# An attention and squared-ReLU kernel: seven products in place of eight for the second half batch and for the last two token tiles, and turned distance blocks as weights

## The chip, the cores and the metric

The kernel runs on one core of one Trainium2 chip. A core has five engines with a queue each: PE (TensorE, matrix products into PSUM; its weight loads are shown apart as PEld), DVE (VectorE), ACT (ScalarE), POOL (GpSimd, which here only issues transfers) and SP (SyncE, which issues transfers too). The metric is the device time of one launch in microseconds. A measurement is the median of several executions; one more execution is profiled, and its trace is what the views below are read from.

## What is computed

Attention with a linear distance penalty, a local window of 96 positions and 8 global keys, and behind it a feed-forward layer with a squared ReLU. 4 batches, 8 heads of 64, 768 positions, 2048 hidden columns:

```python
scores = q @ k.T / 8 - slopes[h] * dist          # dist: |i - j|, 96 for a global key outside the window
scores = where(is_global | is_local, scores, -1e9)
a = softmax(scores)
x = (a @ v) with the heads side by side          # 3072 x 512
h = maximum(x @ w_in, 0)                         # 3072 x 2048
out = (h * h) @ w_out                            # 3072 x 512
```

## The kernel before

**Halves.** The work is cut into eight half batches of 384 tokens (`halves[0]` to `halves[7]`, three token tiles of 128 each). Each goes through attention, which leaves the turned tokens `x.xt` (512 x 384), then the first layer, which leaves the squared hidden values `x.h2` (16 hidden tiles of 128 x 384), then the second layer. Halves 0 and 1, the first batch, are worked through tile by tile in an opening of their own (`OPENING`, a list of short names: `P` distances, `S` scores, `A` attend, `X` turn into `x.xt`, `F`/`G` first layer of half 0, `E`/`D` of half 1). All later halves run their attention beside the two layers of the half before.

**Scores of the first batch.** For the first three tiles `distances` (line 1391) lays the penalty into PSUM ahead of the scores: for each of 8 heads a matmul with a scaled identity `slope_id` as weights and a 128-column block of `dmask16` as the moving side. `score_tile` adds the scores on top, and one exponential follows. For the other tiles the exponential is multiplied with a ready `mask` on DVE.

**Seven products in place of eight.** From half 2 on the first layer is computed in groups (`layer1_group`, line 913): two input blocks of 256 rows, two halves of 192 tokens, and two sets of two hidden tiles (m and m+8) make a 2 x 2 by 2 x 2 block product, done with seven products of four 192-column matmuls instead of eight. Four groups cover the 16 hidden tiles; `LETTERS` and `LAYER1` say in which order their products stand. For this, sums of w_in blocks are made once (`list_in_mix`, line 876, which needs all four chunks of w_in), sums of token blocks for each half (`list_x_mix`, line 898), and in between PSUM banks are copied out or handed from one product to the next: three copies (the one into a second bank, `seed`, and two `hold`), two relus and two `add_relu` for each group. The second layer does the same with two token tiles together (`layer2_pair`, line 1117): seven products of eight 256-column matmuls, with sums of hidden tiles (`mix_tokens`, line 1074, whole or in two parts by `WIDE`) and of w_out blocks (`list_mix`, line 561).

In the kernel before, half 0 and half 1 do the first layer plainly (`layer1`), half 1's second eight hidden tiles at 384 columns each. Of the 24 token tiles, 22 go in 11 pairs; the first tile of half 0 and the last of half 1 go plainly (`layer2`, line 1049: 16 matmuls of 512 columns each).

**What sets the order.** Every operation is put on record in a `Plan` with the operations that it needs, and `ORDER`, a table written out, says on which engine and at which place each one is issued: `p12` is the PE job with index 12, `l` a load on POOL, `a`, `d`, `g`, `s` any other operation on ACT, DVE, POOL or SP. Engines work through their own queues in that order, and waits between engines are put in by the framework from the data. `LOADING` says in which order the loads of the first batch and of w_in (`c0` to `c3`, 512 hidden columns each) are put on record; `ORDER` has the last word. Each of the eight PSUM banks is given out by the plan.

The pairs and the second layer of half 0 and half 1 are listed in the loop at line 1594:

```python
if hb == 1:
    main = l1(x1, range(8, NFT)) + l2(w, 0)
    pairs = [((w, 1), (w, 2)), ((x, 0), (x, 1))]
...
if hb == 1 and GROUPS:
    side.append((8 * 0.65, list_in_mix))
if hb == 1:
    for i, job in enumerate(l2(x, 2)):
        main.insert(len(main) - 3 + i, job)
```

Of the kernel before, what the change touches and what calls it, by code (L numbers as in the profile page):

```python
# [14 lines left out]
P = 128  # L15
# [3 lines left out]
K4 X11 A20 X00 K5 X10 A21 S4o S4b S3b X21 X20 F1 G11 V2 S5o V3 S5b G10 F0 A40 V4 A30 G01 A41  # L19
A31 G00 G30 X41 F3 X30 X31 A50 X40 F2 A51 E11 G31 G20 X50 G21 X51 E01 E10 D0 E00 D1"""  # L20
# [3 lines left out]
LOADING = """v1 k3 k2 q2 v0 q3 q4 q5 k5 v2 k4 c1 v3 c0 v4 v5 c3 c2"""  # L24
# [12 lines left out]
WIDE = [0, 1, 1, 1, 0, 1, 1, 1, 0, 0, 0]  # L37
# [3 lines left out]
LAYER1 = {2: "abcdAeBfCgD1E2F3G4h5i6j7klmn", 3: "abcdAeBfCgD1E2F3G4h5i6j7klmn",  # L41
# [7 lines left out]
ORDER = """d1 g2 a4 s8 p0 s10 a6 d12 a0 d13 l2 l1 a18 l3 d3 a30 d17 d15 d20 l4 a25 d14 a29 d9 a16 l0 d19 a26  # L49
d22 d21 d5 a23 p2 a28 l10 d11 p1 a24 p5 d7 l5 p3 l6 p10 d31 a32 a33 d34 l9 p6 a27 d35 p9 a39 p8 l8  # L50
d44 p11 d36 a40 p7 d43 l7 p4 a46 p13 d37 a41 p14 d45 l11 p12 d48 a42 p16 p17 d59 a47 l12 p15 a52 p25
d51 p19 l13 a49 d38 p28 p24 d55 a53 p20 l14 d69 p23 d64 a50 p34 d65 a60 l16 p31 d56 p21 a81 p22 d72
p27 l15 a61 p29 d58 p30 a57 p26 d70 a82 p33 l17 d68 p18 a71 a77 p35 d66 l23 p36 p32 d54 a86 d67 a85
p40 d62 p39 l18 d63 a97 d91 a73 p41 l19 d84 a78 d83 a74 p37 d79 l20 a98 d75 p44 l22 p38 d107 l21 d80
p47 d76 a89 p52 p48 d96 l27 a92 d111 p42 a93 l28 d106 a112 p43 l29 a119 p46 a113 d105 p45 a101 l30
d110 p53 d103 p55 p50 a120 p59 a90 d95 d116 a87 d100 p51 d99 d94 p57 d122 p54 d125 p65 p63 p49 d135
d121 p67 d146 a114 d128 a102 p61 p62 a104 d132 d117 a88 p75 d108 a129 p83 d115 a142 d109 p60 d209
a143 d118 d189 p64 a130 d273 d193 a138 p70 a136 p72 d159 p82 a133 d194 p71 d187 a134 p56 d160 a131
d190 a162 p69 d137 a186 p81 d161 l33 a123 d212 p74 d139 a165 d163 l25 a188 d156 p84 d205 a166 l31
d151 p73 a169 a184 d157 p85 l35 d206 a164 d167 a171 d147 p58 a168 l36 d196 p80 d124 l34 a126 p89  # L60
d148 p88 a181 p86 l32 d210 a202 d150 a182 p76 l24 d158 a170 d183 p77 a172 l26 d152 p87 a203 d174
a199 l37 p78 d154 a197 p79 p66 d204 a200 l38 a127 d207 p68 d185 a178 d149 a179 p90 a140 d180 p91
a213 d208 a175 d144 p94 a173 d201 a176 p92 d153 s220 d237 p100 a215 d195 a155 p102 s221 d211 d238
a214 p96 a224 d177 p95 a241 a141 p98 d225 p104 a216 s198 d226 p93 p97 a246 d223 a217 s227 a218 p103
d230 d222 p99 s231 a245 d240 p110 d239 p108 s219 l43 p111 a256 d244 a249 l44 p106 a257 d259 a250
d236 l40^227 p109 d247 p116 d228 p101 a252 l45 d251 a269 d258 p115 l41 a270 p114 d242 p113 a253 d192
l42 a262 d255 p117 a265 d232 p105 l46 d191 a272 a260 d233 p123 a266 l48^220 p118 a263 d280 p121 p122
d235 a274 l39 d234 p132 a278 d268 p128 a145 d279 p130 a287 d264 p126 a292 p127 d271 p125 a290 s327
p134 a285 d267 p139 d286 p135 d283 p133 a302 p136 s248 l47 d254 a295 p129 d296 s328 p143 a288 d293
p141 a284 p138 d297 p142 d304 p140 a289 p124 d300 s229 p137 a303 d294 p120 a306 d281 p146 a305 p144  # L70
d277 p147 a311 p131 a301 d307 p107 s282 d298 a329 p145 d291 p148 a309 p112 a308 d312 a399 d314 p151
p152 d313 p156 l51^282 s299 a330 p149 d310 p119 d315 a331 d322 a341 p150 s243 d316 a333 s261 l49^231
d275 a342 p168 d317 p165 a321 l52 a334 p153 d318 p155 a355 l53 a336 d332 p154 a337 d323 l50 d319
a359 p170 d324 l54 p160 d320 a361 p172 a350 p174 d338 a364 p161 p163 d366 a351 p164 a326 p176 d325
d340 p166 d436 p158 d369 a354 d335 a339 p169 a347 d356 p178 a367 p157 d360 p159 a371 d343 a344 p171
d348 a345 p181 d353 p180 s402 l56^327 a362 p182 a375 d374 p173 a372 p184 d346 p186 s403 a365 p162
d376 a357 p188 a382 d352 p192 d363 a380 p167 p179 a385 d391 s276 p175 s377 a373 p189 d358 a368 p190
a404 p185 d386 p193 s392 d388 d381 p183 p191 d393 a387 p187 l63 d389 p196 a383 p177 d390 a413 l59
p194 d378 a370 d384 a414 l74 p201 d379 a409 p202 p195 a423 l58 p199 d405 a426 d415 l62 p198 a427
d406 a424 d395 l55^377 p206 a410 d407 p200 a437 d416 l61^403 a421 d396 p211 a411 d408 p197 a420 l60  # L80
d397 p203 d481 p212 a417 d429 p204 a422 l75 d425 a445 a418 d484 p207 l66 d412 p205 a444 a438 d433
l57 a430 p213 d428 p216 d435 a446 d400 p220 l65 s434 a431 p214 p219 a455 d447 p215 a454 p227 d450
a448 s496 p222 d398 p225 d485 p218 a449 d486 p217 a461 d432 p210 a464 s497 a452 d419 a458 p224 d482
p231 a401 d460 p228 p229 d465 s349 l64 p221 a442 a453 p226 d466 p235 d456 p232 a462 p223 d469 a475
p239 d483 a451 d467 a571 p234 d459 a457 p208 p233 d473 a489 p237 a494 p209 d470 s474 a471 p230 d439
p241 a468 d440 a498 p242 s394 d478 s443 a500 s441 d463 p236 p238 d476 p249 a479 d472 p245 p244 a517
p240 d488 a501 d487 a505 p247 d499 a506 d477 l73^441 s495 a508 p246 d513 a518 d492 l71 d480 a509
p258 p248 d490 a533 l70 d511 p243 d519 p251 a514 l69 d491 a515 d520 p252 a502 p265 l72 p262 d542
a503 p260 p253 a538 l67 d536 p270 a525 p266 d507 a527 p267 l68 a543 d510 p257 a528 p268 d548 a532
p255 p271 d544 a530 p261 d493 a549 p273 d545 a546 p259 d537 p269 a552 p274 d534 p275 d516 p264 p276  # L90
a540 d547 p278 a556 p272 d554 a553 p254 a550 d535 s575 p250 a551 d559 d504 p282 s576 d521 p283 a565
p279 d523 a529 p281 a524 p277 d522 a563 p284 p286 d566 d560 p287 d568 a578 a567 d557 p280 p291 a564
d541 s558 d555 p263 d577 p285 p256 s526 d561 s512 p293 d583 a531 d569 p295 d595 a602 d539 p296 p292
a604 d570 a605 p298 d598 a596 a607 s597 p288 d599 s562 a608 p290 d606 p294 a585 d601 a586 p301 s574
d579 a592 d600 s573 a603 p297 a617 d609 p289 d614 p303 a588 d610 s584 d587 a593 s572 p306 a611 d580
d619 p307 a612 d623 p299 a589 d663 p310 p308 a615 d582 a624 d613 p300 d664 a625 p304 a629 p315 d590
a616 p312 d591 a621 p323 d581 d631 a635 p309 p302 a645 d627 p311 a618 p329 d630 p316 a628 p319 d594
p317 a636 p313 d640 p327 d637 a632 p305 a653 p321 d638 a650 p333 d622 a642 p322 p330 a644 d659 p320
p318 d654 p314 s660 a639 p325 d633 p326 a648 p332 d634 p335 s626 d658 s655 p324 d649 p331 d646 p334
p336 d656 a661 d641 a643 p328 p346 a667 d668 p351 a651 d682 p338 d657 a698 a692 d670 p353 d669 p355  # L100
d671 p357 d703 p337 a706 d665 a652 p361 d701 p350 a674 d711 p347 a672 p359 a673 d666 p363 p339 d708
d693 a697 p358 a647 p340 d707 a713 a662 p354 d677 p364 d675 p349 d683 a715 p342 s676 d702 d684 p352
p356 d699 a696 p362 p367 d687 a712 p365 d678 s688 p360 d704 a716 s620 p343 d714 a709 d710 p371 d679
p369 d685 p341 d705 d724 a719 p366 a689 d680 p368 a686 d717 p372 a700 p345 d720 d725 p370 d718 a691
p373 a721 p344 d737 d727 a726 d681 p348 d722 p374 d723 p383 d738 a728 p385 d756 a729 p377 a690 d733
p375 a741 d740 a759 d734 p378 d739 d694 d735 s695 p380 d730 d752 d736 p376 d742 d748 p379 d749 a731
d751 s732 d753 p381 p388 d754 p387 p386 a743 d744 a762 d755 a761 d745 p382 s746 p390 d747 p391 d760
p384 d765 d750 d764 p394 s766 a757 p389 a771 a772 s758 p392 d763 p393 d767 d769 s768 s770"""
# [190 lines left out]
def kernel(  # L299
# [1385 lines left out]
```

## Time and profile before

| | us |
|---|---|
| median of three runs (lowest, highest) | 200.09 (199.86, 200.77) |
| the profiled execution | 200.26 |
| its span, first to last instruction | 198.5 |
| PE busy | 190.9 |
| DVE busy | 178.7 |
| ACT busy | 153.6 |

The span is what the trace covers; the rest of the profiled execution lies around it. "Busy" is the union of an engine's instructions, without waiting and without issuing transfers. On PE, matmuls overlap one another, so the time that one takes is longer than its step to the next; a row "us, what xcount" of the chain divided by its count gives the step. On DVE and ACT, the mean time of an instruction holds a drain of about 0.1 us that overlaps the next one where they stand back to back.

### The profile page before, as it was taken

To read this page: it belongs to the slowest core of one execution; us is meant where nothing else is said; L and a number is where in the kernel's file an instruction comes from. 1 tells how busy PE (TensorE), PEld (TensorE's weight loads), DVE (VectorE), ACT (ScalarE), POOL (GpSimd) and SP (SyncE) were. 2 spreads that over 40 slices of the span, in tenths; PEclk is the share of its full clock that TensorE was granted. 3 is DMA by queue.
4 is the path that set the end of the run, shared out by engine and by line. 5 is a ranking of instruction groups with operands and counts; after the bars stand their busy time and mean duration, and the time that the engine had idled before them with its cause. 6 is when DMAs were issued, how large, how long until landed. Compare 5 with 4: busy or idle time off the path is not lost.

```text
span 198.5 us, 6069 instructions
## 1 busy us (share of the span) xinstructions
PE 190.9 (96%) x2428; PEld 166.7 (84%) x2428; DVE 178.7 (90%) x445; ACT 153.6 (77%) x332; POOL 66.6 (34%) x82
## 2 busy tenths in 40 slices
PE   7997999999999999999999999999999999999992
PEld 2775988866987897799989997999889998999992
DVE  7898898999998999998999997999999998898842
ACT  6798766989897989999999987976599758366210
POOL 8996544098006900920696000910000000000000
PEclk9999999999999999999999999999999999999999
DMA  5999999999999999998999996999542050120223
GB/s 160 178 148 191 196 183 170 207 196 155 137 211 125 126 135 271 175 142 138 180 149 150 134 195 166 84 105 156 153 129 81 3 132 5 53 106 3 106 82 132
DMA packets 106604, 27.53 MB, mean 139 GB/s; under 512 B 96720, under 2 KB 103632, under 8 KB 106576
## 3 DMA queue, kind: packets, MB, share of 16 engines
q0 software_dynamic: 74944, 13.11, 86.0%
q1 hardware_dynamic: 30432, 13.45, 33.9%
q10 hardware_dynamic: 1200, 0.59, 1.1%
q8 instruction: 19, 0.31, 0.7%
q14 instruction: 9, 0.07, 0.1%
HBM read 27.26 MB, written 6.29 MB: 169 GB/s over the span
## 4 chain that ended last, share of the span: by engine, by line
PE 83%; DMA 5%; POOL 4%; DVE 4%; ACT 1%; issue 1%; POOLq 0%; DVEq 0%
PE yps L1143 32%; PE hps L929 28%; PE hps L818 9%; PE sp L708 4%; PE av L769 4%; DMA w_mix<-in_k_dram 4%; PE yps L1059 4%; POOL w_mix L488 2%; DMA xt<-tm 2%; POOL v L488 1%; DVE tm L1471 1%; DVE vb L354 1%; PE trp L646 1%; DVE hr L990 1%; POOL sk L488 1%
## 5 line engine op out<-in xcount | busy, mean ns | idle before, releaser
L1143 PEld LDWEIGHTS <-h 128*128 128x128 f16 x376 | 33.9, 98 | 4.1
L721 ACT ACTIVATE ex<-sp 128x512 f16<-128x512 f32 x66 | 35.6, 615 | 1.5 <-PE sp L708 1.3
L929 PEld LDWEIGHTS <-w_in_sb 128*128 128x128 f16 x384 | 32.4, 98 | 2.1 <-issue 0.5
L1143 PEld LDWEIGHTS <-mixed 128*128 128x128 f16 x272 | 25.3, 98 | 3.0
L488 POOL DMA_DIRECT2D v<-in_v_dram x24 | 21.5, 921 | 16.5 <-DMA xt<-tm 16.2
L990 DVE CUSTOM_DVE_ANT_0 hr<-hps,kept 128x384 f16<-128x384 f32 x48 | 25.2, 553 | 1.4 <-ACT y L352 0.5
L929 PEld LDWEIGHTS <-in_mix 128*128 128x128 f16 x288 | 24.3, 98 | 0.6 <-DVE x_mix L908 0.3
L488 POOL DMA_DIRECT2D sq<-in_q_dram x19 | 17.0, 900 | 21.9 <-DMA q<-sq 20.3
L488 POOL DMA_DIRECT2D sk<-in_k_dram x19 | 17.1, 907 | 20.9 <-DMA xt<-tm 11.7
L818 PE MATMUL hps<-xt,w_in_sb 128*128 128x256 f16 (+2 forms) x224 | 23.4, 258 | 0.0
L929 PE MATMUL hps<-xt,w_in_sb 128*128 128x192 f16 x192 | 22.8, 246 | 0.2 <-DMA xt<-tm 0.2
L996 ACT ACTIVATE hr<-hps 128x384 f16<-128x384 f32 x35 | 17.0, 496 | 7.6 <-PE hps L929 7.1
L352 ACT COPY y<-yps 128x256 f32<-128x256 f32 (+2 forms) x36 | 12.9, 369 | 12.7 <-PE yps L1143 12.5
L352 ACT COPY kept<-hps 128x384 f32<-128x384 f32 x41 | 19.0, 491 | 4.6 <-PE hps L929 3.9
L1143 PE MATMUL yps<-w_mix,h 128*128 128x256 f16 (+1 forms) x192 | 22.6, 264 | 0.0
L929 PE MATMUL hps<-x_mix,w_in_sb 128*128 128x192 f16 x192 | 22.1, 246 | 0.3 <-DVE hr L990 0.3
L1143 PE MATMUL yps<-w_out_sb,h 128*128 128x256 f16 (+1 forms) x184 | 22.4, 268 | 0.0
L1143 PE MATMUL yps<-w_mix,mixed 128*128 128x256 f16 (+1 forms) x184 | 22.2, 268 | 0.0
L929 PE MATMUL hps<-x_mix,in_mix 128*128 128x192 f16 x192 | 21.9, 246 | 0.0
L745 DVE TENSOR_TENSOR phat<-ex,mask 128x1024 f16<-128x1024 f16 (+1 forms) x36 | 20.9, 597 | 0.3 <-ACT ex L721 0.3
L818 PEld LDWEIGHTS <-w_in_sb 128*128 128x128 f16 x224 | 17.7, 98 | 3.6 <-DMA w_in_sb<-in_moe_w_in_dram 0.2
L1012 ACT ACTIVATE h<-hr 128x768 f16<-128x768 f16 x23 | 19.3, 846 | 0.1
(112 smaller groups left out, 378.5 us busy)
## 6 DMA issues: line engine op xcount, KB each, us to landing
out_dram<-y SPq DMA_DIRECT2D x23, 256.0 KB, 2.5
v<-in_v_dram POOLq DMA_DIRECT2D x24, 128.0 KB, 6.4
sk<-in_k_dram POOLq DMA_DIRECT2D x19, 128.0 KB, 5.4
sq<-in_q_dram POOLq DMA_DIRECT2D x19, 128.0 KB, 5.9
w_in_sb<-in_moe_w_in_dram POOLq DMA_DIRECT2D x4, 512.0 KB, 11.2
w_out_sb<-in_moe_w_out_dram POOLq DMA_DIRECT2D x4, 512.0 KB, 10.7
y<-in_k_dram ACTq DMA_DIRECT2D x2, 256.0 KB, 4.9
y<-in_q_dram SPq DMA_DIRECT2D x2, 256.0 KB, 4.3
```

Source lines behind the costliest of these rows:

```text
L352: nc.scalar.copy(out=out, in_=in_)
L488: dma = nc.gpsimd.dma_start(out=dst, in_=src[x.b, :, r0 + t * P:r0 + (t + 1) * P, :] .rearrange("h p d -> p h d"))
L708: nc.tensor.matmul(sp[h][:, i, :], lhsT=lhsT, rhs=x.q[rows, r % HT, a, :], start=i == 0, stop=True, skip_group_check=True)
L721: nc.scalar.activation(out=st["ex"][:, h], in_=sp[h], func=AF.Exp, scale=scale)
L745: eng(e).tensor_tensor(out=x.phat[a][:, :, t0:t0 + n], op=ALU.mult, in0=st["ex"][:, :, i0:i0 + 2 * n].rearrange("p e (t b) c -> p e t (b c ...
L769: nc.tensor.matmul(av[:, h, j, :], lhsT=lhsT, rhs=rhs, start=h == 0 and (j, before) == blocks[0], stop=before or r == 0, skip_group_check= ...
L818: nc.tensor.matmul(st["ps"][:, i * n:(i + 1) * n], lhsT=w_in_sb[:, kk, m * P:(m + 1) * P], rhs=x.xt[:, kk, c0:c1], start=i == kk == 0, sto ...
L929: nc.tensor.matmul(st[name][:, i * HC:(i + 1) * HC], lhsT=left(i, kk), rhs=right(kk), start=fresh > 0 and i == kk == 0, stop=kk == KK - 1, ...
L990: nc.vector._custom_dve(TENSOR_ADD_SAT, out=hidden(which)[:, :, cols], in0=sums(name), in1=st[kept], s0=LARGEST, s1=0.0)
L996: nc.scalar.activation(out=o, in_=i, func=AF.Relu)
L1012: nc.scalar.activation(out=h2, in_=hr, func=AF.Square)
L1143: nc.tensor.matmul(st[bank_name][:, 0:n], lhsT=a(m), rhs=b(m)[:, cols], start=fresh > 0 and m == 0, stop=m == HK - 1, skip_group_check=not ...
```

## The change

Four things change together:

1. **Half 1, second eight hidden tiles** (4 to 7 and 12 to 15): groups 3 and 2, seven products of four 192-column matmuls each, in place of eight plain tiles at 384 columns. So the w_in sums and half 1's token sums are listed ahead of that.
2. **Second layer**: three pairs in place of two pairs and two plain tiles, so all 24 token tiles go in 12 pairs.
3. **Distances**: the three 128 x 128 blocks of `dmask16` are turned once on PE and copied to `dmask_t`; then a block is the weights, and the scaled identities of four heads are one 512-column moving side: 2 matmuls in place of 8 for each of five calls.
4. **A new order table**, with the chunks of w_in loaded in another order (2, 0, 3, 1 in place of 1, 0, 3, 2) and half 1's opening covering hidden tiles 0 to 3 and 8 to 11 in place of 0 to 7.

```diff
-A31 G00 G30 X41 F3 X30 X31 A50 X40 F2 A51 E11 G31 G20 X50 G21 X51 E01 E10 D0 E00 D1"""
+A31 G20 G10 X41 F1 X30 X31 A50 X40 F3 A51 E01 G11 G30 X50 G31 X51 E21 E00 D2 E20 D0"""
...
-LOADING = """v1 k3 k2 q2 v0 q3 q4 q5 k5 v2 k4 c1 v3 c0 v4 v5 c3 c2"""
+LOADING = """v1 k3 k2 q2 v0 q3 q4 q5 k5 v2 k4 c0 v3 c2 v4 v5 c1 c3"""
...
-WIDE = [0, 1, 1, 1, 0, 1, 1, 1, 0, 0, 0]
+WIDE = [0, 0, 1, 1, 1, 0, 1, 1, 1, 0, 0, 0]
...
-LAYER1 = {2: "abcdAeBfCgD1E2F3G4h5i6j7klmn", 3: "abcdAeBfCgD1E2F3G4h5i6j7klmn",
+LAYER1 = {1: "abcAdBeCfDgEFG", 2: "abcdAeBfCgD1E2F3G4h5i6j7klmn", 3: "abcdAeBfCgD1E2F3G4h5i6j7klmn",
...
-ORDER = """d1 g2 a4 s8 p0 s10 a6 d12 a0 d13 l2 l1 a18 l3 d3 a30 d17 d15 d20 l4 a25 d14 a29 d9 a16 l0 d19 a26
+ORDER = """g2 s8 a4 d1 p0 a6 s10 d12 a0 d22 l1 d13 l2 a17 l3 d15 a31 l5 a21 a19 d14 a9 d16 d18 p1 d5 a24 d3 d20
...
+    dmask_t = phat_p.tile([P, H, P], FP16, name="dmask_t", tag="ex", bufs=4)
...
+    def turn_dist():
+        st = {}
+
+        def emit(e):
+            st["ps"] = ps = bank([P, 3, P], FP16, "trd")
+            for i in range(3):
+                nc.tensor.transpose(out=ps[:, i], in_=dmask16[:, i * P:(i + 1) * P], identity=ident)
+
+        def turned_dist(e):
+            copy(e, dmask_t[:, 0:3], st["ps"])
+        job = plan.pe(3 * 0.056, emit, [slope_ops[0]], 1)
+        return plan.after(job, {"ACT": 0.4, "DVE": 0.31}, turned_dist)
...
-            for a in range(NPAIR):
-                for h in range(2):
-                    nc.tensor.matmul(pair[h][:, a, :], lhsT=slope_id[:, 2 * a + h, :],
-                                     rhs=dmask16[:, c0:c0 + P], start=a == 0, stop=False,
-                                     skip_group_check=True)
-        st["job", before] = plan.pe(H * (0.066 if r < 2 else 0.056), emit, slope_ops, 2)
+            slope = slope_id.rearrange("p (a h) c -> p h a c", h=2)
+            for h in range(2):
+                nc.tensor.matmul(pair[h], lhsT=dmask_t[:, c0 // P, :], rhs=slope[:, h], start=True,
+                                 stop=False, skip_group_check=True)
+        st["job", before] = plan.pe(2 * 0.22, emit, slope_ops, 2)
...
         if hb == 1:
-            main = l1(x1, range(8, NFT)) + l2(w, 0)
-            pairs = [((w, 1), (w, 2)), ((x, 0), (x, 1))]
+            list_in_mix()
+            list_x_mix(x1)
+            main = l1_mixed(x1)
+            pairs = [((w, 0), (w, 1)), ((w, 2), (x, 0)), ((x, 1), (x, 2))]
...
-        if hb == 1 and GROUPS:
-            side.append((8 * 0.65, list_in_mix))
-        if hb == 1:
-            for i, job in enumerate(l2(x, 2)):
-                main.insert(len(main) - 3 + i, job)
```

What the new table does on each engine, as the two programs' orders stand side by side: on PE 32 matmuls of 384 columns and 32 of 512 fall away, 56 of 192 and 56 of 256 come; the first pair's first product stands behind fewer matmuls of the first layer than before. On POOL the first eleven loads are again tiles of k, q and v in another order, the first chunk of w_in is again the twelfth load; the sixth v tile now stands ahead of the third w_in chunk, and a v tile of half 2 stands between the second and the third chunk of w_out. The last product on PE is now one of the second-to-last pair, with 256 columns; before, it was one of the last pair with 128.

More of the change, by code (lines that the diff above doesn't have):

```diff
@@ L54 @@
[L54 to L80, printed above, removed]
@@ L111 @@
+d793 s794 p395 d791 p390 d787 s792 a781 s782"""
 class Op:
@@ L896, in list_in_mix, with x_parts @@
                 in_mix_ops[g] = made
+    def x_parts(x, pairs):
+        return [o for a in pairs for o in (
+            [x.x_ops[a]] if a in x.x_ops else [x.x_ops[a, t] for t in range(HT)])]
     def list_x_mix(x):
         b = lambda k, n: x.xt[:, k * KK:(k + 1) * KK, n * HC:(n + 1) * HC]
-        first, second = [x.x_ops[a] for a in range(KK)], [x.x_ops[a] for a in range(KK, NCT)]
+        first, second = x_parts(x, range(KK)), x_parts(x, range(KK, NCT))
         x.t_ops = []
@@ L954, in plain @@
             return (lambda kk: x.xt[:, k * KK + kk, n * HC:(n + 1) * HC],
-                    [x.x_ops[a] for a in range(k * KK, (k + 1) * KK)])
+                    x_parts(x, range(k * KK, (k + 1) * KK)))
         def mixed(k):
@@ L1524, in l1_mixed @@
         own = [g for g in GROUPS if LETTERS[g][0] in order]
-        plain = l1(x, [m for m in ALTERNATE if m % (NFT // 2) // 2 not in own])
+        plain = l1(x, [m for m in ALTERNATE if m % (NFT // 2) // 2 not in own]) if x.hb > 1 else []
         groups = {g: layer1_group(x, g) for g in own}
@@ L1560 @@
                            rank=0) for h in range(H)]
+    slope_ops.append(turn_dist())
     mask_ops = [plan.add({"ACT": 0.43}, lambda e, h=h: fill_mask(h), [dist_op], rank=10 + h)
```

94 lines of the change are left out of this document (61 added, 33 removed).

## Prediction, before the changed kernel ran

> **What bounds the kernel now.** I read the page first (share of each engine, chain), then busy time by stretches, then the chain in order of time, then groups by form, and last the landings of single transfers.
>
> ```profile
> span 198.5 us, 6069 instructions
> ...
> PE 190.9 (96%) x2428; PEld 166.7 (84%) x2428; DVE 178.7 (90%) x445; ACT 153.6 (77%) x332; POOL 66.6 (34%) x82
> ...
> PE 83%; DMA 5%; POOL 4%; DVE 4%; ACT 1%; issue 1%; POOLq 0%; DVEq 0%
> ```
>
> TensorE holds 83% of the chain. A busy PE need not be a PE at its pace, so the stretches come next (columns: PE, PEld, DVE, ACT and POOL busy, granted clock, DMA share, GB/s).
>
> ```profile
> 20.00:36.00 16.00, 15.81 (x204) 14.11 (x204) 14.39 (x44) 11.05 (x24) 7.35 (x9) 1.00 1.76 185
> 36.00:50.00 14.00, 14.00 (x164) 9.86 (x163) 13.65 (x36) 13.39 (x31) 9.63 (x11) 1.00 1.77 183
> 50.00:66.00 16.00, 16.00 (x208) 13.57 (x206) 14.82 (x34) 13.84 (x29) 5.13 (x6) 1.00 1.59 152
> 66.00:80.00 14.00, 14.00 (x194) 12.21 (x193) 13.63 (x34) 13.21 (x29) 4.08 (x6) 1.00 1.70 184
> 80.00:100.00 20.00, 20.00 (x265) 17.95 (x265) 19.10 (x43) 19.26 (x42) 9.51 (x12) 1.00 1.32 159
> ...
> 120.00:140.00 20.00, 19.76 (x256) 18.09 (x251) 18.78 (x43) 15.73 (x35) 6.12 (x7) 1.00 1.20 126
> ...
> 160.00:180.00 20.00, 19.66 (x212) 18.54 (x210) 17.87 (x42) 12.98 (x27) 0.00 (x0) 1.00 0.21 64
> ```
>
> From 36 to 120 us PE never idles, at full clock. DVE and ACT are nearly as full: from 20 to 100 us DVE is busy 75.6 of 80 us (14.39+13.65+14.82+13.63+19.10) and ACT 70.8. So matmul time taken out there shortens the run only as far as DVE and ACT can follow. That is the whole question here.
>
> **Matmuls removed and added.** The pace of each form, from the chain in order of time (start, us, what):
>
> ```profile
> 29.04 0.50 PE av L1456 x16
> ...
> 36.30 0.67 PE trp L646 x12
> ...
> 41.34 0.65 PE hps L818 x4
> 42.00 0.86 PE yps L1059 x4
> ...
> 50.09 5.24 PE yps L1143 x48
> ...
> 66.78 6.93 PE hps L929 x84
> ```
>
> That is 56 ns for 128 columns (0.67/12), 162 for 384, 215 for 512, 109 for 256, 82 for 192, and 31 for the 65 of attention.
>
> - Half 1, hidden tiles 4 to 7 and 12 to 15: 8 tiles x 4 matmuls of 384 columns go, 32 x 162 = 5.2 us. Two groups come: 14 products x 4 matmuls of 192 columns, 56 x 82 = 4.6 us. **-0.6 us.**
> - Second layer: the two plain token tiles go, 32 matmuls of 512, 32 x 215 = 6.9 us. A twelfth pair comes: 7 products x 8 matmuls of 256, 56 x 109 = 6.1 us. **-0.8 us.**
> - Distances: 40 matmuls of 128 columns (2.2 us) become 10 of 512 (2.2 us) plus three transposes (0.17 us). The order of the changed program agrees: 10 of 512 with the turned blocks as weights. Nothing gained in columns, and all of it lies before the first first-layer product, which waits for something else:
>
> ```profile
> 20.03 1.93 PE L818 MATMUL hps<-xt,w_in_sb 128*128 128x256 f16 x24
> ...
> L818 PEld LDWEIGHTS <-w_in_sb 128*128 128x128 f16 x224 | 17.7, 98 | 3.6 <-DMA w_in_sb<-in_moe_w_in_dram 0.2
> ```
>
> The first layer (line 818) starts at 20.03 us, and of its weight loads one waited for a chunk of w_in, 0.2 us: the start hangs on that landing. In the changed order the same eleven tiles of k, q and v stand ahead of the first chunk, so I cost the opening at 0 with bounds -0.3 and +0.8: the turned block adds a transpose and a copy ahead of the first distances, and the landing covers them; if that cover fails, about the 0.4 us of that copy and the 0.17 us of transposes show, and more if a wait is late too.
>
> Sum on TensorE: **-1.4 us.**
>
> **Work that comes to DVE and ACT.** Groups by form (busy us and mean ns of one):
>
> ```profile
> L990 DVE CUSTOM_DVE_ANT_0 hr<-hps,kept 128x384 f16<-128x384 f32 x48 | 25.2, 553 | 1.4 <-ACT y L352 0.5 <-PE hps L929 0.4 <-ACT ex L721 0.2
> L352 ACT COPY kept<-hps 128x384 f32<-128x384 f32 x41 | 19.0, 491 | 4.6 <-PE hps L929 3.9 <-DVE hr L990 0.6
> L996 ACT ACTIVATE hr<-hps 128x384 f16<-128x384 f32 x35 | 17.0, 496 | 7.6 <-PE hps L929 7.1
> L1206 DVE TENSOR_TENSOR y<-yps,y 128x256 f32<-128x256 f32 x22 | 9.0, 421 | 4.9 <-PE yps L1143 4.6 <-ACT ex L721 0.2
> L908 DVE TENSOR_TENSOR x_mix<-xt 128x384 f16<-128x384 f16 x12 | 4.2, 353 | 1.0 <-DMA xt<-tm 0.7 <-PE hps L929 0.4
> L1110 DVE TENSOR_TENSOR mixed<-h 128x512 f16<-128x512 f16 x10 | 4.2, 420 | 0.7 <-ACT h L1012 0.7
> L352 ACT COPY yps<-yps 128x256 f32<-128x256 f32 x10 | 3.7, 369 | 1.6 <-PE yps L1143 1.4
> L847 ACT ACTIVATE hr<-hps 128x384 f16<-128x384 f32 x6 | 2.8, 526 | 0.0
> L354 DVE COPY y<-yps 128x512 f32<-128x512 f32 x1 | 0.7, 685 | 0.0
> ```
>
> Each new group: three copies (0.49), two relus (0.50), two adds (0.55). Two groups: 6 x 0.49 + 4 x 0.50 + 4 x 0.55 = 7.1 us, less the 8 plain relus (8 x 0.53 = 4.2): +2.9. The squares stay as many. Mixing half 1's tokens: 4 x 0.35 = +1.4. The twelfth pair, one of those in two parts: 8 token sums x 0.42 = 3.4; five copies x 0.37 and two adds x 0.42 = 2.7; less two plain copies (1.4): +4.7. Together **+9.0 us**, all between about 30 and 80 us. Part of that is only a drain that the next instruction overlaps:
>
> ```profile
> 62.88 3.04 ACT L721 ACTIVATE ex<-sp 128x512 f16<-128x512 f32 x6 [0.34 <-PE sp L708]
> ...
> L721 ACT ACTIVATE ex<-sp 128x512 f16<-128x512 f32 x66 | 35.6, 615 | 1.5 <-PE sp L708 1.3
> ```
>
> Six in a row take 0.51 each against a mean of 0.62. With 0.1 us saved on each of the some 20 more instructions, 7 us of engine time are added. Also the first w_in sums move some 4 us earlier and the w_out sums ahead of an earlier first pair; they are no new work.
>
> Room: from 20 to 100 us DVE and ACT now idle 4.4 + 9.2 = 13.6 us. The stretch gets 1.4 us shorter, which takes 2.8. Left: 13.6 - 7 - 2.8 = 3.8 us on two engines over 78.6 us. Both would be 97.6% busy, against (19.10+19.26)/40 = 96% in the stretch quoted from 80 to 100, where PE lost nothing. So 96% is not a ceiling, but 97.6% is not seen. I cost this at 0, since the order table places every instruction anew and spreads copies between the two engines (the changed order has 9 more relus of a group on ACT, 5 fewer on DVE); the bound is +1.4 us, worked out below.
>
> **Order and transfers.** The w_in chunks are needed in another order, and the last v tile now stands ahead of the third chunk. In before the third chunk comes first and that v tile behind it; with the two exchanged, the chunk lands when the tile landed, issued at 15.3 us, 12.3 later, at 27.6.
>
> ```profile
> L488 POOL DMA_DIRECT2D v<-in_v_dram x1: 926/926/926, 15.3 to 15.3; - x1
> ...
> DMA to landing us min/median/max: 12.3/12.3/12.3
> ...
> 26.41 0.39 PE L1486 MATMUL trx<-ident,tm 128*128 128x128 f16 x4
> 26.99 0.29 PE L1486 MATMUL trx<-ident,tm 128*128 128x128 f16 x2 [0.19 <-DVE tm L1471]
> ```
>
> Ahead of the chunk's first use stand, by the paces above, 7.1 us of matmuls: wanted at 27.15, there at 27.6: a wait of 0.5 us. The wait of before (four transposes end their issue at 26.63, the next begin at 26.99: 0.36 us) stands at another place and is gone. **+0.1 us.** The idle 0.24 and 0.34 us of PE in the stretches from 120 and 160 stand at places that the new table writes anew; I take half as gone, **-0.3**, bounds -0.6 and +0.6.
>
> **The end.** The last product is now one of 256 columns of the pair before the last, its copy on ACT (0.37), its store 256 KB. Of before (timeline, then issues with KB and us to landing):
>
> ```profile
> 194.25 0.61 PE L1143 MATMUL yps<-w_mix,h 128*128 128x128 f16 x8
> 194.90 0.29 DVE L354 COPY y<-yps 128x128 f32<-128x128 f32 x1
> 195.40 0.38 SPq L1225 DMA_DIRECT2D out_dram<-y  x1
> ...
> out_dram<-y SPq DMA_DIRECT2D x23, 256.0 KB, 2.5
> ...
> out_dram<-y SPq DMA_DIRECT2D x1, 64.0 KB, 1.9
> ```
>
> Copy +0.08, landing up to +0.6: I take **+0.3**.
>
> **Sum.** -1.4 + 0.1 - 0.3 + 0.3 = -1.3. The profiled execution took 200.26 us (span 198.5), 0.17 above the median of 200.09. So 199.0 for it, and **198.8 us** as the median.
>
> **A rule against it.** Each matmul here brings its own weight load, and there are more and shorter matmuls after the change (56 of 192 and 56 of 256 for 32 of 384 and 32 of 512).
> If a load, 98 ns by the row of line 818, set the pace wherever a matmul is shorter, 192 columns would cost 98 in place of 82: 56 x 16 = 0.9 us of the gain lost, 199.7 us. The chain row of 84 such matmuls in 6.93 us speaks against it. [...]
>
> **The rivals.**
> - *DVE and ACT set the pace* from 20 to 100 us. For: 97.6% needed, 96% seen. Against: PE idled nowhere in that stretch after 36 us, so their ceiling is not shown. Price: now 75.6 + 70.8 us, with the new 7 us 153.4; at 96% of both, 79.9 us in place of 78.6: +1.3. **200.1 us.**
> - *The w_out sums come too late* (the slower side). The first pair starts some 6.5 us earlier (50.1 before, by its chain row; after, 20.0 + 23.5 us of matmuls by the paces above), but w_out is loaded no earlier, and a v tile stands ahead of its last two chunks. Before, the last chunk was issued at 32.1 and took 13.2 us:
>
> ```profile
> L556 POOL DMA_DIRECT2D w_out_sb<-in_moe_w_out_dram x1: 740/740/740, 32.1 to 32.1; - x1
> ...
> DMA to landing us min/median/max: 13.2/13.2/13.2
> ```
>
> Landing 45.3; the v tile (128x512 f16, 131 KB) at the 183 GB/s of the stretch from 36 us is 0.7 us more, so 46.0; the DVE instruction that wants it should come up at about 47. If it lands after 47, DVE stands still, in order, with token sums, masks and adds behind it, and PE follows us for us. From 47 + 2.3 on the run is slower by over 0.5%: 2.3 more on 198.8, or 1 us here on top of the first rival's 1.3. **201.2 us.**
> - *The weight load sets the pace* of the short matmuls, as worked out above: **199.7 us.** The rows speak against it.
>
> **Chances.** Forecast 0.56 (its own range 198.0 to 199.6, from the bounds of order, opening and end; about a fifth of it above 199.1). First rival 0.26, second 0.16, third 0.02. A measurement of this kernel tells about 0.5%, 1.0 us, from no change. Faster by more (below 199.1): 0.45 of the forecast's 0.56, and 0.03 of the first rival, where only a part of its price is due: 0.48. Slower by more (above 201.1): 0.14 of the second rival, 0.02 of the first where both come together: 0.16. Within: the rest, 0.36. The range for 8 in 10 goes from the forecast's lower bound to between the first two rivals: 198.0 to 200.8.
>
> **What would show it.** PE busy from 20 us to the end down by 1.4, L929 at 82 ns and L1143 at 109, no L1059. DVE and ACT busy from 20 to 100 us up by 7 to 9 in sum; if ACT or DVE release PE waits there (chain pieces of DVE hr, ACT kept or tm), the first rival holds; if DVE waits for w_out at 44 to 48 us, the second. A wait of PE for w_in near 27 us of about 0.5. The last store after an ACT copy. Wrong from the ground would be: another pace of 192 columns, or a first-layer start off 20.0 by over 0.8.

## The result, and the profile after

The changed kernel takes **203.25 us** (202.93 to 203.47), the kernel before 199.98: a ratio of 1.0146 (1.012 to 1.0173; such a bracket behind a ratio is its 95% interval). It is 1.5% slower; the forecast was 198.8 us, the range 198.0 to 200.8. The profiled execution took 203.47 us, 3.21 more than the one of before. Ratios leave out executions that took over 1.5% longer than the fastest of the same kernel.

First the page of the kernel after: span, busy time of each engine, and the chain's shares.

```profile
span 201.7 us, 6139 instructions
...
PE 191.6 (95%) x2449; PEld 168.7 (84%) x2449; DVE 178.9 (89%) x456; ACT 159.5 (79%) x345; POOL 66.7 (33%) x82
...
PE 70%; DVE 14%; DMA 9%; ACT 3%; issue 2%; POOL 0%; SPq 0%; DVEq 0%; POOLq 0%; ACTq 0%
```

Of the chain, PE had 83% and DVE 4% before. Now DVE has 14% and transfers 9%: on the way to the end, something waits for DVE that did not before. The busy time by stretches (columns as in the prediction) says where:

```profile
20.00:36.00 16.00, 15.97 (x239) 14.65 (x239) 14.94 (x47) 15.59 (x33) 8.23 (x10) 1.00 1.75 184
36.00:60.00 24.00, 24.00 (x310) 21.58 (x308) 23.37 (x62) 23.23 (x54) 8.77 (x10) 1.00 1.63 186
60.00:80.00 20.00, 19.60 (x281) 17.48 (x280) 18.30 (x45) 19.53 (x45) 10.55 (x13) 1.00 1.82 149
80.00:100.00 20.00, 19.59 (x267) 17.86 (x265) 19.55 (x46) 19.20 (x43) 9.31 (x11) 1.00 1.54 173
100.00:120.00 20.00, 19.73 (x264) 17.86 (x262) 18.09 (x47) 15.83 (x37) 7.28 (x9) 1.00 1.65 164
120.00:140.00 20.00, 19.86 (x254) 17.84 (x252) 18.42 (x41) 17.36 (x38) 5.15 (x6) 1.00 0.94 109
140.00:160.00 20.00, 18.54 (x241) 16.85 (x238) 17.95 (x44) 14.30 (x29) 0.10 (x1) 1.00 0.42 98
```

PE idles 0.4 us in each of the two stretches from 60 to 100, where it never did, and 1.5 us from 140 to 160. The losses are larger than these idle times, because a matmul counts as busy for longer than its step to the next (246 ns on average for 192 columns, by the page, against a step of 82). So I also counted the loss in another way: for each matmul, the start of the next less its own start less the step of its form (56, 82, 109, 162, 216 ns and so on), summed from the first product with w_in to the last. Small extra times at the edges of the score bursts (the groups of score matmuls, 64 rows in place of 128) are in it too: where PE doesn't wait, the step into each of the 16 bursts is 96 to 98 ns longer, and the step out of it takes 147 to 149 ns, in both kernels.

| profiled execution | before | after | difference |
|---|---|---|---|
| first product with w_in at | 20.03 | 20.92 | +0.89 |
| matmuls from there on, at their steps | 168.88 | 167.47 | -1.41 |
| loss from there to 100 us | 2.87 | 4.08 | +1.21 |
| loss from 100 us to the last product | 2.92 | 5.38 | +2.46 |
| last product's end to the span's end | 3.79 | 3.85 | +0.06 |
| together | | | +3.21 |

The matmul work, counted at its steps, shrank by the 1.4 us that were worked out, and 4.6 us came back as waiting. The largest part of it lies after 100 us, in stages in which the change adds no work at all.

What waits there? DVE's waits from 20 to 180 us (us in total, times, longest), the kernel before and then the one after:

```profile
DVE x_mix L908 <- DMA xt<-tm: 0.7, 1, 0.7
```

```profile
DVE x_mix L928 <- DMA xt<-tm: 4.1, 4, 1.7
```

The sums of token blocks (`x_mix`) wait for the transposed tokens of their half batch (`xt`), a transfer that SP issues. The timeline of after around the worst of these waits, with the rows of SP, DVE and PE that make it:

```profile
133.63 0.56 DVE L797 TENSOR_TENSOR tm<-av,rec 128x384 f16<-128x384 f32 x1
...
134.38 1.67 SPq L680 DMA_TRANSPOSE q<-sq  x1
...
136.10 0.88 SPq L1249 DMA_DIRECT2D out_dram<-y  x1
...
137.09 0.54 SPq L618 DMA_DIRECT2D vb<-v  x1
...
137.68 0.60 SPq L619 DMA_DIRECT2D vb<-v  x1
...
138.40 1.72 SPq L812 DMA_TRANSPOSE xt<-tm  x1
...
143.25 0.36 DVE L928 TENSOR_TENSOR x_mix<-xt 128x384 f16<-128x384 f16 x1 [1.75 <-DMA xt<-tm]
...
143.86 0.42 DVE L1226 TENSOR_TENSOR y<-yps,y 128x256 f32<-128x256 f32 x1
...
144.33 0.49 PE L1163 MATMUL yps<-w_mix,h 128*128 128x256 f16 x3 [0.94 <-DVE y L1226]
```

Read from the top: the tokens are ready at 134.2. SP is free of the q transpose at 136.05, but a store of the output and two copies of values stand next in its queue, and the transpose of the tokens is issued only at 138.40. DVE reaches the sum at 141.5 and stands still until 143.25. Behind the sum, in DVE's queue, stands the add that frees the accumulator PE needs next, so PE stands too. At 97 us the same happens with two stores, which hold the transpose for 1.1 us:

```profile
94.83 1.56 SPq L812 DMA_TRANSPOSE xt<-tm  x1
96.44 1.04 SPq L1249 DMA_DIRECT2D out_dram<-y  x2
...
97.58 1.30 SPq L812 DMA_TRANSPOSE xt<-tm  x1
...
103.43 0.36 DVE L928 TENSOR_TENSOR x_mix<-xt 128x384 f16<-128x384 f16 x1 [1.54 <-DMA xt<-tm]
```

This transpose also took the longest of all twelve to land, 5.8 us after its issue began, so not the whole wait of 1.54 is SP's queue.

In the kernel before, the two transposes of that half went out back to back, and the next stores came behind them. But it had such a place of its own further on (its timeline):

```profile
94.38 2.57 SPq L796 DMA_TRANSPOSE xt<-tm  x2
...
117.81 2.26 SPq L1229 DMA_DIRECT2D out_dram<-y  x2
...
120.17 1.26 SPq L796 DMA_TRANSPOSE xt<-tm  x1
```

Its one wait of DVE for `xt`, the 0.7 us above, ended at 123.36 us, when this transpose had landed, and PE lost 0.37 us there. The new table sends these two out back to back (117.78 us) and puts stores and copies ahead of two others.

### The profile page after: what moved, and what is told of

The parts are those of the page before. It is cut to its first block, busy times and chain, and to the rows that moved or that the text cites. A ratio compares the mean times of both kernels' runs of the same rounds, so it can differ in the third digit from the quotient of the medians.

```text
span 201.7 us, 6139 instructions
## 1 busy us (share of the span) xinstructions
PE 191.6 (95%) x2449; PEld 168.7 (84%) x2449; DVE 178.9 (89%) x456; ACT 159.5 (79%) x345; POOL 66.7 (33%) x82
## 4 chain that ended last, share of the span: by engine, by line
PE 70%; DVE 14%; DMA 9%; ACT 3%; issue 2%; POOL 0%; SPq 0%; DVEq 0%; POOLq 0%; ACTq 0%
PE yps L1163 28%; PE hps L949 24%; PE hps L834 8%; DMA xt<-tm 7%; PE av L785 3%; PE sp L724 3%; DMA q<-sq 2%; ACT mask L449 2%; DVE hr L1010 2%; DVE phat L761 1%; DVE vb L356 1%; DVE tm L1490 1%; DVE mixed L1130 1%; DVE h L1034 1%; PE sp L1425 1%
## 5 line engine op out<-in xcount | busy, mean ns | idle before, releaser
L1163 PEld LDWEIGHTS <-h 128*128 128x128 f16 x408 | 37.4, 98 | 5.1 <-issue 1.1
L1010 DVE CUSTOM_DVE_ANT_0 hr<-hps,kept 128x384 f16<-128x384 f32 x52 | 27.7, 550 | 1.0 <-PE hps L949 0.7
L1016 ACT ACTIVATE hr<-hps 128x384 f16<-128x384 f32 x44 | 21.6, 508 | 8.0 <-PE hps L949 7.9
L354 ACT COPY kept<-hps 128x384 f32<-128x384 f32 x49 | 23.3, 501 | 3.9 <-DVE hps L356 2.2
L1163 PE MATMUL yps<-w_out_sb,h 128*128 128x256 f16 (+1 forms) x200 | 25.1, 268 | 0.0
L1163 PE MATMUL yps<-w_mix,mixed 128*128 128x256 f16 (+1 forms) x200 | 24.8, 268 | 0.0
L354 ACT COPY y<-yps 128x256 f32<-128x256 f32 (+1 forms) x35 | 13.0, 377 | 14.6 <-PE yps L1163 14.4
L949 PE MATMUL hps<-x_mix,in_mix 128*128 128x192 f16 x208 | 24.2, 246 | 0.1
L1032 ACT ACTIVATE h<-hr 128x768 f16<-128x768 f16 x25 | 21.7, 874 | 1.5 <-DVE mixed L1130 1.0
L761 DVE TENSOR_TENSOR phat<-ex,mask 128x1024 f16<-128x1024 f16 (+1 forms) x36 | 21.1, 593 | 0.4 <-ACT ex L737 0.4
L834 PE MATMUL hps<-xt,w_in_sb 128*128 128x256 f16 (+1 forms) x192 | 17.8, 246 | 0.0
```

Of the source, the lines that this page charges most:

```text
L354: nc.scalar.copy(out=out, in_=in_)
L761: eng(e).tensor_tensor(out=x.phat[a][:, :, t0:t0 + n], op=ALU.mult, in0=st["ex"][:, :, i0:i0 + 2 * n].rearrange("p e (t b) c -> p e t (b c ...
L834: nc.tensor.matmul(st["ps"][:, i * n:(i + 1) * n], lhsT=w_in_sb[:, kk, m * P:(m + 1) * P], rhs=x.xt[:, kk, c0:c1], start=i == kk == 0, sto ...
L949: nc.tensor.matmul(st[name][:, i * HC:(i + 1) * HC], lhsT=left(i, kk), rhs=right(kk), start=fresh > 0 and i == kk == 0, stop=kk == KK - 1, ...
L1010: nc.vector._custom_dve(TENSOR_ADD_SAT, out=hidden(which)[:, :, cols], in0=sums(name), in1=st[kept], s0=LARGEST, s1=0.0)
L1016: nc.scalar.activation(out=o, in_=i, func=AF.Relu)
```

## The experiments

Two theories stood against each other. **A**: the new table puts some instructions and transfers at places where a queue, worked in order, waits for a late transfer. **B**: the added DVE and ACT work has used up the slack, and the waits are only where the backlog shows. Edits of the table are shown as the words of one engine's queue, in order.

**e1, the token sums later** (DVE's words).

```diff
-d254 d266
+d266 d254
...
-d347 d359
+d359 d347
...
-d421 d431 d439 d424 d432
+d431 d439 d424 d432 d421
...
-d603 d633 d619 d634 d585 d563
+d633 d619 d634 d585 d563 d603
```

> Four token sums of the changed kernel (those before which VectorE stood idle for a transposed-token transfer: 0.6 us at 63, 0.2 at 82, 1.5 at 103 and 1.8 at 143) are issued one to five VectorE instructions later; nothing else moves. Theory A (VectorE, in order, waits for a late transfer, and PE waits for what is queued behind): the 4.1 us of waiting fall below 1, the PE losses of 0.9 us at 105 to 111 and of 2.0 at 143 to 147 go, 200.5 us. Theory B (the added work has used up the slack of VectorE and ScalarE; the wait is only where the backlog shows): PE still loses at these places, 202.8 us or more.

Measured: ratio 1.0055 (1.0023 to 1.0086), 1.8 us better than the changed kernel. DVE's wait for `xt` fell to 0.6 us, the loss after 100 us from 5.38 to 3.47. By the waits A holds; the time, 201.58 us, lies about halfway between its 200.5 and B's 202.8. PE now lost 0.36 us at 81.6, in part waiting for a sum that came later.

**e3, two v loads behind the q and k loads** (POOL's words).

```diff
-l41 l39 l43 l42 l44^244
+l41 l43 l42 l44^244 l39
...
-l52 l55 l54^251 l49^352 l51
+l52 l54^251 l49^352 l51 l55
```

> In the changed kernel two loads of v tiles that stand between the loads of q and k tiles for half batches 4 and 5 go behind the last of these. Theory A' (the q and k transfers set the score bursts at 77 and 96 us, where PE loses 0.57 us each time): both losses go, about 0.9 us faster, 202.3 us. Theory B (backlog on VectorE and ScalarE): what PE gains there it loses at the next place that waits for VectorE, 203 us.

Measured: ratio 1.0059 (1.0027 to 1.0092). No wait for q was left at 77 and 96 us, and the loss up to 100 us was 3.35 in place of 4.08. A later run (e2: 3.37) shows that this part also changes without the edit, so that gain can't be told from scatter. The late part fell too, to 3.80, and DVE's wait for `xt` to 1.8 us, though neither SP's order nor DVE's was touched: the late loss varies by itself.

**e4, the first loads nearly as before** (POOL's words).

```diff
-l1 l2 l3 l5 l4 l9 l0 l10 l6 l7 l8
+l1 l2 l3 l5 l4 l0 l10 l6 l9 l8 l7
```

> In the changed kernel the first eleven loads are put so that the last k tile is the 10th and the last q tile the 11th, as before the change, and the third v tile the 9th in place of the 6th. If the landing of the last k tile sets the start of the first layer (PE waited 0.75 us for it at 18.3), the first product with w_in starts at about 20.0 in place of 20.9 and the run takes 202.4 us. If VectorE's queue sets it, the start stays within 0.3 us of 20.9. If the start moves but the slack theory B holds, the gain is lost later and the run takes 203 us.

Measured: ratio 1.0123 (1.0087 to 1.0159), first product at 20.90. The start didn't move, but PE now waited 0.8 us for the last q tile where it had waited 0.7 for the last k tile. So this run does not tell DVE's queue from a landing.

**e5, the added work alone, in the kernel before.**

```diff
         def relu(e):
...
+            for _ in range(2 if x.hb == 1 and n == HALF else 1):
...
             def square(e):
...
+                for _ in range(2 if x.hb == 1 and n == HALF else 1):
...
                 def token_sum(e, k=k, c=c, ms=ms):
...
+                    for _ in range(2 if one == (halves[0], 1) and k < 2 else 1):
```

> The kernel before, with the relus and squares of half 1's 384-column tiles and the first two token sums of the first pair's parts each issued twice (16 more instructions, about 7 us of ScalarE and VectorE time between 36 and 52 us; TensorE, the order and the transfers as before). Theory B (7 us more of such work costs what the changed kernel lost): 203 us or more. Theory A (the work fits in, the loss came from the order and the transfers): 201 us or less.

Measured: ratio 1.0304 (1.0236 to 1.0373), 6.3 us slower, clearly on B's side. From 20 to 200 us PE waited for these (first two rows of its waits):

```profile
PE sp L708 <- ACT hr L848: 2.6, 4, 0.8
PE av L769 <- DMA v<-in_v_dram: 2.0, 1, 2.0
```

The score bursts wait for PSUM banks that ACT's doubled relus give back late, and 2 us go when a v load comes late after that. Dropped into a finished order, this work (8.5 us more of DVE and ACT busy by the page) cost 6. So the order that absorbs such work has to be made for it, and this run can't say whether the new table is one.

**e6, three edits together**: e1, e3, and on SP the edit that e2, below, has alone.

> The changed kernel with three edits of its table: the four token sums issued later and the two v loads behind the q and k loads, each of which alone took 1.7 and 1.4 us off, and on SP the two transposes of tokens that stood behind stores of the output (97.6 and 138.4 us) ahead of them. If the edits remove different losses: 200.0 us or less. If both shorten the same wait (VectorE's for the transposed tokens, which shrinks from 4.1 to 1.1 and 1.8 us in the two alone): about 201.2 us.

Measured: ratio 1.0021 (1.0007 to 1.0035). The loss after 100 us fell to 2.40, below that of the kernel before; but PE now waited 0.6 us at 70 for a v load that e3 had put too far back, and 0.5 at 81 behind a token sum that e1 had.

**e7, twelve squares left out of the changed kernel.**

```diff
         def hidden(which):
+            if x.hb in (1, 2):
+                return x.h2[:, m0 + which * far:m0 + which * far + 2]
...
             def square(e):
+                if x.hb in (1, 2):
+                    return
```

> The changed kernel without the twelve squares of the groups of half batches 1 and 2 (relus write straight to the hidden tiles, the output is that of a plain ReLU for these); the same order and transfers otherwise. This takes about as much VectorE and ScalarE time out as the change put in, between 40 and 85 us. Theory B (the added work has used up the slack): VectorE is ahead again at 100 us, the PE losses from 100 to 147 us shrink from some 3 to 1, 201 us or less. Theory A (the order and late transfers): VectorE only waits longer for the transposed tokens at 101 and 141 us, 202.7 us or more.

Measured: 201.73 us, ratio 1.0086 (1.0054 to 1.0117), 1.2 us better than the changed kernel, for 5.8 us less of DVE and ACT busy by the page (6.1 us is what the change had added). The loss after 100 us was 4.02. The time lies between the two theories. DVE's wait for `xt` fell to 1.5 us, where A had it grow; and PE now lost most in front of a score burst at 137 us, for a q transpose; the changed kernel has no such loss there:

```profile
PE sp L724 <- DMA q<-sq: 1.4, 2, 1.2
```

So part of what the smaller work gave may have gone there, and this run decides for neither.

**e8, a copy of values later** (DVE's words).

```diff
-d92 d72 d69 d59 d73 d71 d63 d87 d86
+d72 d69 d59 d73 d71 d63 d87 d86 d92
```

> The changed kernel with the copy of the third block of values (two DVE copies, 1.05 us at 17.0) issued behind the last copies that the first product with w_in waits for. If VectorE's queue sets the start of the first layer: 20.2 in place of 20.9 us, 202.5 us in all if the gain lasts. If a k or q tile's landing sets it: no earlier than 20.6.

Measured: ratio 1.0131 (1.0079 to 1.0183). The first product came at 20.55, but PE lost 0.43 at 23.6, where DVE now has the copy to do and the normalised tokens come late, and 1.3 at 79 to a token transfer. No gain.

**e9, e6 and e8 together.**

> The edits of the three-edit kernel and the later copy of values together: the sum of both gains, 199.3 us or less, if they are independent; if an earlier start only makes VectorE and ScalarE the later bound, the same time as the three-edit kernel within 0.3 us.

Measured: ratio 1.0034 (1.0007 to 1.0061), first product at 20.22: the same as e6.

**e2, the two transposes ahead on SP, alone** (SP's words).

```diff
-s401 s284 s300 s416
+s401 s416 s284 s300
...
-s600 s467 s597 s582
+s600 s582 s467 s597
```

> The changed kernel with only the two transposes of tokens on SP (97.6 and 138.4 us) ahead of the stores of the output, and of the copies of values, that stood before them. If their place on SP is why VectorE waited for them at 102 and 142 us: they land 1 to 2 us earlier, both waits (1.5 and 1.8 us) fall below 0.5, about 1.5 us faster, 201.7 us. If the transfer itself is late for another reason (its tokens, or the load on the DMA engines): less than 0.5 us.

Measured: ratio 1.0002 (0.9968 to 1.0035). Two words moved on SP, and nothing else on any engine, take 2.9 us off (2.4 against the second measurement of the changed kernel, e13), twice what I had put down for it and nearly the whole difference. SP's rows and the DVE sum in the timeline of this kernel:

```profile
131.77 1.67 SPq L680 DMA_TRANSPOSE q<-sq  x1
...
133.55 1.55 SPq L812 DMA_TRANSPOSE xt<-tm  x1
...
135.15 0.57 SPq L1249 DMA_DIRECT2D out_dram<-y  x1
...
135.82 0.54 SPq L618 DMA_DIRECT2D vb<-v  x1
...
139.89 0.35 DVE L928 TENSOR_TENSOR x_mix<-xt 128x384 f16<-128x384 f16 x1
```

The transpose follows the q transpose at once, and the sum has no wait in brackets. The one at 97 us now goes out at 95.3, and its sum has none either. In all, DVE waits 0.5 us for `xt`:

```profile
DVE x_mix L928 <- DMA xt<-tm: 0.5, 1, 0.5
```

The loss after 100 us is 2.51 in place of 5.38, below the 2.92 of the kernel before; 1.8 us of this came off between 140 and 150 us, mostly where PE had stood behind the add. The loss up to 100 us is 0.7 lower as well, though the edit touches nothing before 93 us: that much is scatter.

**e10, mended**: e6 and e8, with `l39` behind two loads only, `d347` at its old place, and one copy out of PSUM earlier.

```diff
-d607 d615 d620
+d607 d620 d615
```

> The four-edit kernel, with what its profile showed still late: one of the two v loads goes behind two loads in place of four (PE waited 0.6 us for it at 70), one of the four token sums stays where it was (0.5 at 81), and one copy out of PSUM goes ahead of a mask product (0.33 at 144). If these are the places: 0.9 us off the 200.85 of the four-edit kernel, 199.6 to 200.0 us, a little below the kernel before. If the work leaves no room, other stalls come in their place: 200.4 or more.

Measured: 200.02 us beside 200.48 of the kernel before, ratio **0.9965 (0.9934 to 0.9996)**: the best of all that compute the whole function, no more than just clear of no change, and with some 0.7 us about half of the 1.3 that the prediction summed up. Its page:

```profile
span 197.1 us, 6138 instructions
...
PE 189.8 (96%) x2449; PEld 168.5 (85%) x2449; DVE 178.7 (91%) x456; ACT 159.0 (81%) x345; POOL 66.8 (34%) x82
...
PE 87%; DMA 3%; POOL 3%; DVE 3%; ACT 1%; issue 1%; POOLq 0%
```

PE has 87% of the chain again. The loss is 3.31 up to 100 us and 1.96 after; in its first-layer start (20.46) it is still 0.4 behind the kernel before.

**e12, e10 without the twelve squares.**

> The mended kernel without the twelve squares of the groups of half batches 1 and 2 (7.3 us of VectorE and ScalarE time; relus write straight to the hidden tiles, the output is that of a plain ReLU for these). In the changed kernel as it stood this gave about 1.2 us. If the added work still costs by itself once the table is mended: 1 us or more below the mended kernel. If only the places mattered: within 0.4 us of it.

Measured: 199.61 us, ratio 0.9959 (0.9928 to 0.9991). Beside 200.02 of e10 on the same chip, 5.5 us less of DVE and ACT busy are worth 0.4 us, no more than either kernel scatters. But its profile has a loss of 1.2 us in front of the score burst at 137 us, as in e7, that e10 doesn't have:

```profile
PE sp L724 <- DVE h L1134: 1.0, 1, 1.0
```

So in this kernel no cost of the added work shows, and up to about 1.2 us of it may be hidden by that wait.

**e11, the distances as before, in the changed kernel.**

```diff
-            slope = slope_id.rearrange("p (a h) c -> p h a c", h=2)
-            for h in range(2):
-                nc.tensor.matmul(pair[h], lhsT=dmask_t[:, c0 // P, :], rhs=slope[:, h], start=True,
-                                 stop=False, skip_group_check=True)
+            for a in range(NPAIR):
+                for h in range(2):
+                    nc.tensor.matmul(pair[h][:, a, :], lhsT=slope_id[:, 2 * a + h, :],
+                                     rhs=dmask16[:, c0:c0 + P], start=a == 0, stop=False,
+                                     skip_group_check=True)
```

> The changed kernel with the distances laid down as before the change: 40 matmuls of 128 columns with the scaled identities as weights in place of 10 of 512 with the turned blocks (the three transposes and their copy stay in). By the steps of 56 and 216 ns both take 2.2 us of PE: no difference, 203.3 us within 0.5. If the four-to-one number of weight loads matters in the opening: the first product with w_in 0.5 us later or more, 203.8 us.

Measured: ratio 1.0175 (1.0121 to 1.0229), no difference to the changed kernel that could be told (its interval is 1 us to either side); first product at 20.70. Its profile shows something else. PE lost 0.85 us at 60 and 2.56 at 77.6, before two score bursts:

```profile
PE sp L724 <- DMA q<-sq: 3.1, 2, 2.4
```

and in turn only 2.48 after 100 us, with SP's order as in the changed kernel. DVE did not wait for the transposed tokens at all: it reached the two sums at 104.08 and 142.16 us, 2.2 and 0.7 us later than in the changed kernel, and the second transpose landed 3.4 us after its issue began, in place of 4.8. So in this profile the late loss is gone without any edit on SP: it is the outcome of a race between the engines and a transfer, in which both vary.

**e13, the changed kernel once more.**

> The changed kernel itself, unedited. If the late start and the waits for q at the score bursts belong to its table: first product with w_in after 20.4 us, some 4 us of PE losses from 20 to 100 us and some 5 after 100, a ratio of 1.013 to 1.017. If they are scatter: one of them gone, a ratio below 1.011.

Measured: ratio 1.0122 (1.0042 to 1.0202), 202.03 to 205.25 us, first product at 20.83: a ratio between the two. The profiled execution was the longest of the four, and its losses are not read.

**e14, e2 with the loads of q and k earlier** (`l39` behind two loads, `l55` behind three).

> The kernel with the two transposes ahead on SP (ratio 1.0002), with the two v loads behind q and k loads in addition (one behind two of them, one behind three). If the order of the loads is behind the waits for q at 77 and 96 us: neither shows a wait, PE losses from 20 to 100 us at most 3.2 us, a ratio of 0.997 or less. If the waits are scatter: the same ratio within 0.002.

Measured: ratio 1.0006 (0.9973 to 1.0039), as e2. PE still lost 0.79 at 77, waiting for q. So the place of the v loads doesn't decide that wait.

**e15, e2 with the copy of values later.**

> The kernel with the two transposes ahead on SP, with the copy of the third block of values behind the copies that the first product with w_in waits for in addition. If VectorE's queue is behind the late start: the first product at 20.1 to 20.5 us (20.4 to 21.1 in the runs without this edit) and a ratio of 0.998 or less. If the landing of the last k and q tiles is behind it: 20.6 or later, the same ratio.

Measured: ratio 1.0028 (0.9994 to 1.0061). The first product came at 20.34, but 0.45 went at 23.4 and 1.7 at 79, as in e8.

The runs that carry the verdict, side by side (loss as defined above, of one profiled execution each):

| | first w_in product | loss to 100 us | loss after | ratio |
|---|---|---|---|---|
| before | 20.03 | 2.87 | 2.92 | 1 |
| after | 20.92 | 4.08 | 5.38 | 1.0146 |
| e7, less work | 20.71 | 3.19 | 4.02 | 1.0086 |
| e1, sums later | 20.41 | 3.96 | 3.47 | 1.0055 |
| e3, v loads behind | 20.92 | 3.35 | 3.80 | 1.0059 |
| e4, first loads | 20.90 | 3.52 | 5.67 | 1.0123 |
| e8, values later | 20.55 | 4.60 | 3.78 | 1.0131 |
| e11, old distances | 20.70 | 6.09 | 2.48 | 1.0175 |
| e2, SP's transposes ahead | 21.11 | 3.37 | 2.51 | 1.0002 |
| e14, and loads | 20.84 | 3.71 | 2.12 | 1.0006 |
| e15, and values later | 20.34 | 5.05 | 2.50 | 1.0028 |
| e10, mended | 20.46 | 3.31 | 1.96 | 0.9965 |
| e12, mended, less work | 20.13 | 3.83 | 2.96 | 0.9959 |

Every kernel with the edit on SP (the last five, and e6 and e9) loses less than 3 us after 100 us and has a ratio of at most 1.0034; of the others with the changed table's order of work, only e11 loses so little there, which came late by itself, and none has a ratio below 1.005. For the late loss, A is shown. The edits of e1 and e3 shorten the same wait of DVE for `xt` (from 4.1 us to 0.6 and 1.8; the edit on SP to 0.5), so their gains are not added to that of e2. What the added work costs by itself is not settled: 0.4 us in e12, with up to 1.2 more that may be hidden there.

## Why the prediction was wrong

The step that failed is "The idle 0.24 and 0.34 us of PE in the stretches from 120 and 160 stand at places that the new table writes anew; I take half as gone, -0.3, bounds -0.6 and +0.6". A table written anew can also make new waits, and I bounded those with the size of the old ones. It made 2.46 us of them after 100 us. e2 shows the place: two transposes on SP behind stores and copies. The half that I took as gone was about right: from 120 to 130 and from 160 to 180 us PE lost 0.95 and 0.58 us before, 0.65 and 0.39 after. SP's new order could be read from the changed program as POOL's could; I went through POOL's load by load and priced nothing on SP's but the last store.

Step by step:

- *Matmuls, -1.4 us.* Right: -1.41. The paces held too, in the chain of after (start, us, what):

```profile
112.66 1.98 PE hps L949 x24
...
153.60 0.87 PE yps L1163 x8
```

 that is 82.5 ns for 192 columns and 109 for 256. So the weight load (98 ns by the page of after) does not set the pace of 192 columns, as the third rival (199.7 us) had it: the kernel is slower, but not in these steps.
- *Distances, 0 us.* Right as far as e11 can tell, within 1 us.
- *Opening, 0, bounds -0.3 and +0.8.* Wrong by 0.9, outside its bounds and past the 0.8 that the prediction names as a sign of being wrong from the ground. I had the start hang on the landing of a w_in chunk. The chain of after says otherwise:

```profile
17.35 0.71 DVE vb L356
...
18.38 0.42 DVE tm L1490
18.81 0.33 DVE q L356
...
19.26 0.43 DVE tm L1490
...
19.75 0.29 PE trx L1505 x2
20.03 0.95 PE sp L1425 x24
20.98 0.54 PE hps L834 x4
```

 It hangs on DVE's queue, in which a copy of values now stands ahead, and behind which 24 score matmuls come, as in the kernel before. In the nine profiles read with the changed DVE order there the start is 20.4 to 21.1; with the copy moved it is 20.1 to 20.6 in five. So the copy is some 0.4 us of it. It isn't free to move (e8, e15). The rest of the 0.9 is not settled.
- *Added work: 7 us net, cost 0, bound +1.4.* The amount was about right: from 20 to 100 us DVE and ACT are busy 76.2 + 77.6 us by the stretches above, against 146.4, so 7.4 more, 96.1% of both; over the whole span it is 6.1 (DVE 0.2, ACT 5.9). The cost is open: 6 us in e5, 1.2 by e7, 0.4 by e12, the last two with a wait for something else in the way. It depends on the order, and a busy share doesn't tell it.
- *First rival (DVE and ACT set the pace, 200.1 us).* Not what happened: what PE lost more before 100 us stands in front of score bursts that wait for q, not behind DVE or ACT.
- *Second rival (w_out late, 201.2 us).* Did not happen: none of DVE's waits from 20 to 180 us is for w_out.
- *w_in near 27 us, +0.1.* No such wait shows: the third chunk landed at 27.84 us, and with a start 0.9 later it was there.
- *The end, +0.3.* +0.06.

What stays open, besides the cost of the added work: the 1.2 us that PE lost more before 100 us, at the score bursts of 77 and 96 us. They come and go between kernels with the same order there (losses up to 100 us: 4.08 in the changed kernel, 3.37 in e2, 6.09 in e11), and so does PE's wait for the q transposes (0.8 us, none listed, and 3.1 us in these three). Why the changed order leaves them less room than the one before was not settled.

## What to carry to other kernels

Where every engine's order is written out, price a new order by its queues, not only by its sums: for each transfer that an engine working in order will wait for (here DVE, 1.75 us in front of the sum at 143.25), take the end of its producer, the time that the issuing queue spends on what stands ahead of it (2.3 us ahead of the transpose at 138.40), the landing time (2.8 to 5.8 us), and the place of the consumer. Whatever nobody waits for (stores) goes behind what somebody waits for (2.9 us in e2). A loss that appears far behind the stage that was changed, with the engines no fuller than before, can point to such a queue, as it did here.

## What the runs showed of the hardware

Issuing takes time on SP. In the kernel after, a store took 0.3 to 0.9 us, a copy of values 0.5 to 0.6 in six of seven (1.6 in the other), and a transpose of tokens 1.2 to 2.1, with a median of 1.24. That is no small part of a transpose, which took a median of 4.0 us from the start of the issue to the landing; and the three issues ahead of the one at 138.40 took 2.3 us together. The landings of the twelve transposes of tokens in the kernel after:

```profile
DMA to landing us min/median/max: 2.8/4.0/5.8
```

On DVE nothing passed the waiting instruction: the mask product at 143.53 and the add at 143.86 came behind the sum that had waited 1.75 us. The landing of one and the same kind of transfer varied from 2.8 to 5.8 us within one execution, a spread of 3.0 us where the change was to gain 1.3.
